# Grouping tap products by channel chunk, and adding all tap pairs in the DMA, in a convolution and MLP kernel

## Chip, cores and metric

The kernel runs on one core of one Trainium2 chip. The metric is the device time in microseconds of one execution; lower is better. The time before is the median of three runs.

## What is computed

Each token's 192 channels are split into 8 heads of 24. Every token and head has 7 weights, normalised by a softmax over the 7 taps; a tap is one of the token's own row and the six rows before it. The result goes through a two-layer MLP whose middle function is `h - tanh(h)`:

```python
w = exp(weight_gen - max); w = w / sum(w)                    # B=8, S=4096, H=8, K=7
x_pad = concat([zeros(B, 6, D), x], axis=1)                  # D = 192
x_unf[b, s, k] = x_pad[b, s + k]                             # 7 shifted rows of each token
attn = einsum('bshk,bskhg->bshg', w, x_unf).reshape(B * S, D)
h = attn @ w_in                                              # 192 x 2048
out = (h - tanh(h)) @ w_out                                  # 2048 x 192
```

## The kernel before

The 32768 tokens are cut into 32 blocks of 1024, eight consecutive tokens (`J = 8`) to each of 128 partitions. For each block:

- SP issues the loads of `x_t` (14 rows of 192 channels a partition: eight tokens and a halo of six) and of `wg_t`. ScalarE takes the exponential (L146), VectorE sums it, takes the reciprocal and scales, so that `wsm` holds the softmax.
- `products` (L205) multiplies the shifted rows with the weights, one instruction per tap: 1536 elements a partition, bf16 out. GpSimd does all seven taps of blocks 2 to 31. Taps 0, 2, 4 go to the tile `even`, taps 1, 3, 5 to `odd`, tap 6 to `last`.
- A DMA issued by GpSimd (L241) adds `odd` to `even`. Blocks 0 and 1 (`PLAIN`) have none. In blocks 2 to 6 (`PART`) it adds two tap pairs and is issued after tap 3. In the other 25 blocks it adds three pairs, without the last third of the third pair (`ACC`), and is issued after tap 5.
- `conv_sums` (L260) adds what is left, and transposes it, with matmuls against an identity (L277): 8 matmuls for each chunk of 64 channels and each remaining group. Three chunks with 4, 4 and 5 groups make 104 matmuls in a late block; five groups each make 120 in a `PART` block; seven make 168 in a `PLAIN` one. `conv_out` copies the sums to `convT`, chunks 0 and 1 on ScalarE (L303), chunk 2 on VectorE (L301).
- `gemm1` (L315) makes one of 16 f tiles: 6 matmuls into `ph`, tanh on ScalarE (L333), the subtraction `gt` on VectorE (L334). `gemm2` (L345) makes one eighth of the output of the block before from 32 matmuls into `obank` (L358).

The order on every engine is written out by hand in the program; engines run their own instructions in order. In a steady block n there are eight steps p of two `gemm1` tiles and one `gemm2` part. The products of block n+2 are issued on GpSimd at p = 0, their first instruction held back until the latest `gt` of that time (`behind`, reason "pace"). The sums of block n+1 are made at p = 6, those of chunks 0 and 1 strewn between the `gemm2` matmuls, those of chunk 2 in one burst.

The first two blocks are different. VectorE helps with the taps: the list `taps` names engine, tap and token range. `conv(0, (0, 1), (2,))` (L483) sums the groups in the order of `sums`, so TensorE takes each tap as it comes. `load_x(1, first_halo[0])` (L469) holds the second load of x behind a first product of block 0 that reads halo rows. In the pass of `gemm1` over block 0 the sums of block 1 are interleaved: 48 matmuls, the first three groups of chunks 0 and 1, after f tile 7 (p = 3), then 16 at each of p = 4, 5 and 6, and the rest at the end (L500 to L509). `hooks` puts two loads of MLP weights, issued by GpSimd, behind chosen entries of `taps`.

Of the kernel before, what the change touches and what calls it, by code (L numbers as in the profile page):

```python
# [9 lines left out]
BF16 = mybir.dt.bfloat16  # L10
# [6 lines left out]
def kernel(  # L17
# [8 lines left out]
    nc = tc.nc  # L26

    B, S, D = x.shape
    H, K = weight_gen.shape[2], weight_gen.shape[3]
    G = D // H  # L30
    F = moe_w_in.shape[1]
    P = nc.NUM_PARTITIONS
    R = P // 2
    HALO = K - 1

    J = 8
# [5 lines left out]
    NFT = F // P  # L42
    NC = D // R
    GC = G // NC
    NPAIR = K // 2
    ACC = NPAIR * J * D - J * R
    PLAIN = (0, 1)
    PART = (2, 3, 4, 5, 6)
    assert S % TOK == 0 and D % R == 0 and H * GC == R and F % P == 0
# [5 lines left out]
    ppool = ctx.enter_context(tc.tile_pool(name="ppool", bufs=2))  # L55
# [21 lines left out]
    prods_of = {}  # L77
# [120 lines left out]
    def scale(eng, wsm, e_t, zr):  # L198
        return eng.tensor_mul(  # L199
            wsm.rearrange("p j h k -> p (j h) k"),  # L200
            e_t[:].rearrange("p j h k -> p (j h) k"),
            zr.rearrange("p (n o) -> p n o", o=1).to_broadcast([P, J * H, K]),
        )

    def products(n, taps=None, sums=None, hooks={}, behind=None):  # L205

        x_t = x_of.pop(n)
        wsm, wsm_v, e_t, zr = wsm_of.pop(n)
        if e_t is not None:
            scale(nc.gpsimd, wsm[:], e_t, zr[:])  # L210

        even = ppool.tile([P, NPAIR, NC, J, H, GC], BF16, name="even")
        odd = ppool.tile([P, NPAIR, NC, J, H, GC], BF16, name="odd")
        last = ppool.tile([P, NC, J, H, GC], BF16, name="last")
        dst = {}
        for i in range(NPAIR):
            dst[2 * i] = even[:, i]
            dst[2 * i + 1] = odd[:, i]
        dst[K - 1] = last[:]
        if -1 in hooks:  # L220
            hooks[-1]()
        for eng, k, j0, j1 in taps or [(nc.gpsimd, k, 0, J) for k in range(K)]:
            w = wsm_v if eng is nc.vector else wsm[:]
            mul = eng.tensor_mul(  # L224
                dst[k][:, :, j0:j1].rearrange("p c j h g -> p j h c g"),
                x_t[:, k + j0 : k + j1, :].rearrange("p j (h c g) -> p j h c g", h=H, c=NC),
                w[:, j0:j1, :, k : k + 1]
                .rearrange("p j h (k o) -> p j h k o", o=1)
                .to_broadcast([P, j1 - j0, H, NC, GC]),
            )  # L230
            if k == 0 and behind is not None:


                order(mul, behind, "pace")
            if j1 == 1:
                first_halo[0] = mul
            if (k, n in PART) in ((3, True), (K - 2, False)) and n not in PLAIN:


                acc = 2 * J * D if n in PART else ACC  # L240
                nc.gpsimd.dma_start(  # L241
                    out=even[:].rearrange("p i c j h g -> p (i c j h g)")[:, 0:acc],
                    in_=odd[:].rearrange("p i c j h g -> p (i c j h g)")[:, 0:acc],
                    accum_op=mybir.AluOpType.add,
                    max_dma_last_dim=4096,
                )
            if k in hooks:
                hooks[k]()

        if n in PLAIN:  # L250
            prods_of[n] = [[dst[k] for k in (sums or range(K))]] * NC
        elif n in PART:
            prods_of[n] = [[dst[4], even[:, 0], even[:, 1], dst[5], last[:]]] * NC
        else:
            groups = [last[:]] + [even[:, i] for i in range(NPAIR)]
            prods_of[n] = [
                groups + ([odd[:, NPAIR - 1]] if c == NC - 1 else []) for c in range(NC)
            ]

    def conv_sums(n, parts, pcs, home=None):  # L260


        prods = prods_of[n]
        if n not in conv_of:
            conv_of[n] = cpool.tile([P, NC, HT], BF16, name="convT")
        for _ in parts:
            pcs.append(home or psum_h.tile([P, 2, HT], FP32, name="pc", tag="ph"))

        for gi in range(max(len(g) for g in prods)):
            for chunks, pc in zip(parts, pcs):  # L270
                some = [c for c in chunks if gi < len(prods[c])]
                last = gi == max(len(prods[c]) for c in chunks) - 1
                for c in some:
                    for j in range(JH):
                        col = ((c - chunks[0]) * JH + j) * R
                        for r in range(2):
                            nc.tensor.matmul(  # L277
                                pc[r][:, col : col + R] if home else pc[:, r, col : col + R],
                                lhsT=prods[c][gi][
                                    r * R : (r + 1) * R, c, 2 * j : 2 * j + 2  # L280
                                ].rearrange("p j h g -> p (j h g)"),
                                rhs=ident[r * R : (r + 1) * R, r * R : (r + 1) * R],
                                start=(gi == 0 and c == chunks[0] and j == 0),
                                stop=(last and c == some[-1] and j == JH - 1),
                            )
                            yield
# [22 lines left out]
    def conv(n, *parts):  # L309
        pcs = []  # L310
        for _ in conv_sums(n, parts, pcs):
            pass
        conv_out(n, parts, pcs)
# [127 lines left out]
    def rest_of_w_in():  # L441
        load_w_in(FA, F)

    V, G_ = nc.vector, nc.gpsimd
# [4 lines left out]
    load_w_in(0, FA, last_exp[0])  # L449
    softmax_norm_ramp(0, obank[0])  # L450
    products(
        0,

        taps=[
            (G_, 6, 0, J),
            (V, 5, 1, J),
            (V, 4, 2, J),
            (V, 5, 0, 1),
            (V, 4, 0, 2),
            (G_, 0, 0, J),  # L460
            (V, 3, 0, J),
            (V, 2, 0, J),
            (G_, 1, 0, J),
        ],
        sums=(6, 5, 4, 3, 0, 2, 1),
        hooks={1: rest_of_w_in},
    )

    load_x(1, first_halo[0])  # L469
# [4 lines left out]
    for c in range(NC):  # L474
        nc.scalar.activation(out=w_in[R:P, c, 0:FA], in_=w_in[0:R, c, 0:FA], func=ACT.Copy)
    softmax_norm_ramp(1, obank[1])
    nc.sync.dma_start(out=w_in[R:P, :, FA:F], in_=w_in[0:R, :, FA:F])
    products(
        1,
        taps=[(V, 0, 0, J), (V, 1, 0, J)] + [(G_, k, 0, J) for k in range(2, K)],  # L480
        hooks={4: load_w_out},
    )
    conv(0, (0, 1), (2,))  # L483
    softmax_exp(2)
    load_x(2)
    softmax_norm_ramp(2)
    products(2)

    def some(sums, m):
# [24 lines left out]
    for n in range(1, NTOT):  # L514
# [103 lines left out]
```

The softmax here doesn't subtract the row's maximum and nothing guards it: scores larger than these inputs give would overflow.

## Time and profile before

| quantity | value |
|---|---|
| time, median of three runs (lowest to highest) | 754.1 us (753.81 to 754.71) |
| span of the profiled execution, first to last instruction | 751.8 us |
| TensorE matmul busy | 732.1 us, 97% of the span, 14800 instructions |
| VectorE busy | 695.5 us, 93% |
| ScalarE busy | 625.3 us, 83% |
| GpSimd busy | 670.5 us, 89% |
| mean busy share of the 16 DMA engines, blocks in mid-run | 0.56 to 0.58 |
| granted TensorE clock | 1.000 |

The time of the profiled execution itself is not listed; its span stands 2.3 us under the median of the timed runs, which is what lies around the span in a timed execution. "Busy" adds the times of the instructions of an engine. The page has 40 slices of the span in tenths, the chain of work that ended last, and groups of instructions by line with the mean duration and the idle time ahead of them. The timeline lists start, duration, engine and line.

### The profile page before, as it was taken

Reading aid. Unit: us, or ns where it says so; the run is one execution under the profiler, and the core shown is the slowest. Engines: PE = TensorE matmul, PEld = TensorE weight load, DVE = VectorE, ACT = ScalarE, POOL = GpSimd, SP = SyncE. Lnnn points to the kernel's source line nnn. Section 1 sums busy time; section 2 is a strip of 40 time slices with the busy share of each in tenths; the row PEclk is TensorE's granted clock in tenths of the full one; section 3 lists DMA queues with packets and bytes.
Section 4 is the critical chain, followed back from the end, with each engine's and each line's share of the span. In section 5 each row is a group of like instructions: output and inputs, shape, how many; then the busy total and the mean of one; then the engine's idle time right before and its main releaser. Section 6 shows DMA issues by size and latency. Waiting matters only on the chain.

```text
span 751.8 us, 32359 instructions
## 1 busy us (share of the span) xinstructions
PE 732.1 (97%) x14800; PEld 577.5 (77%) x14800; DVE 695.5 (93%) x740; ACT 625.3 (83%) x840; POOL 670.5 (89%) x264
## 2 busy tenths in 40 slices
PE   3899999999999999999999999999999999999997
PEld 2477878877777778777777778777878777877777
DVE  7999999999999999999999999999999999998893
ACT  4888888888888888888888888888888888888883
POOL 8999999999999999999999999999999999999000
PEclk9999999999999999999999999999999999999999
DMA  8936444465556665555666544666544566542312
GB/s 229 213 79 172 152 149 111 107 186 171 158 161 155 186 184 126 136 151 160 176 186 172 125 130 149 171 184 186 121 125 148 168 186 173 121 115 62 79 45 86
DMA packets 25943, 110.82 MB, mean 147 GB/s; under 512 B 4703, under 2 KB 9551, under 8 KB 21838
## 3 DMA queue, kind: packets, MB, share of 16 engines
q1 hardware_dynamic: 14718, 77.03, 28.3%
q0 software_dynamic: 11088, 31.72, 24.9%
q8 instruction: 115, 1.88, 1.0%
q14 instruction: 22, 0.18, 0.1%
HBM read 54.52 MB, written 25.17 MB: 106 GB/s over the span
## 4 chain that ended last, share of the span: by engine, by line
PE 94%; DVE 4%; DMA 1%; ACT 0%; issue 0%; DVEq 0%
PE obank L358 44%; PE ph L320 43%; PE pc L277 6%; DVE gt L334 2%; PE po L395 1%; DMA x_t<-in_x_dram 1%; DVE odd L224 0%; DMA wg_t<-in_weight_gen_dram 0%; DVE even L224 0%; DVE zsum L160 0%; DVE obank L199 0%; ACT convT L295 0%; ACT e_t L146 0%; DVE obank L188 0%; DVE zr L169 0%
## 5 line engine op out<-in xcount | busy, mean ns | idle before, releaser
L334 DVE TENSOR_TENSOR gt<-ph,th 128x1024 bf16<-128x1024 f32 x512 | 602.5, 1220 | 33.0 <-ACT th L333 30.0
L333 ACT ACTIVATE th<-ph 128x1024 f32<-128x1024 f32 x512 | 497.5, 1022 | 69.4 <-PE ph L320 68.0
L358 PE MATMUL obank<-w_out,gt 64*128 64x192 bf16 x7936 | 412.5, 243 | 0.1
L358 PEld LDWEIGHTS <-gt 64*128 64x128 bf16 x7936 | 357.4, 94 | 55.7 <-issue 0.2
L320 PE MATMUL ph<-convT,w_in 64*128 64x512 bf16 x3072 | 384.9, 378 | 4.8 <-DVE gt L334 2.8
L224 POOL TENSOR_TENSOR even<-x_t,wsm 128x1536 bf16<-128x1536 f32 x93 | 287.6, 3092 | 12.3 <-DVE gt L334 12.1
L224 POOL TENSOR_TENSOR odd<-x_t,wsm 128x1536 bf16<-128x1536 f32 x93 | 287.3, 3089 | 0.0
L320 PEld LDWEIGHTS <-w_in 64*128 64x128 bf16 x3072 | 174.6, 94 | 101.6 <-issue 11.6
L377 ACT ACTIVATE out_sb<-obank 128x192 f32<-128x192 f32 x248 | 82.3, 332 | 35.0 <-PE obank L358 30.5
L224 POOL TENSOR_TENSOR last<-x_t,wsm 128x1536 bf16<-128x1536 f32 x32 | 106.6, 3333 | 0.0
L277 PE MATMUL pc<-ident,even 64*128 64x64 bf16 x2256 | 62.8, 191 | 0.3 <-DVE even L224 0.2
L277 PEld LDWEIGHTS <-even 64*128 64x128 bf16 x2304 | 59.7, 96 | 1.2 <-issue 0.5
L241 POOL DMA_DIRECT2D even<-odd x30 | 36.1, 1205 | 9.3 <-POOL odd L224 9.3
L277 PE MATMUL pc<-ident,last 64*128 64x64 bf16 x752 | 27.2, 191 | 9.3 <-POOL last L224 9.2
L303 ACT ACTIVATE convT<-pc 128x1024 bf16<-128x1024 f32 (+1 forms) x33 | 32.6, 992 | 2.8 <-PE pc L277 2.8
L277 PEld LDWEIGHTS <-last 64*128 64x128 bf16 x768 | 23.2, 96 | 9.6 <-POOL last L224 9.2
L160 DVE TENSOR_REDUCE zsum<-e_t 128x32 f32<-128x224 f32 (+1 forms) x61 | 23.7, 388 | 3.0 <-ACT e_t L146 3.0
L146 ACT ACTIVATE e_t<-wg_t 128x448 f32<-128x448 f32 x32 | 18.5, 578 | 6.7 <-DMA wg_t<-in_weight_gen_dram 6.7
L301 DVE CAST convT<-pc 128x512 bf16<-128x512 f32 x30 | 20.7, 690 | 3.6 <-PE pc L277 1.9
L169 DVE RECIPROCAL zr<-zsum 128x32 f32<-128x32 f32 (+1 forms) x58 | 20.3, 350 | 0.0
L199 DVE TENSOR_TENSOR wsm<-e_t,pc 128x448 f32<-128x448 f32 x28 | 17.4, 622 | 2.9
L277 PE MATMUL pc<-ident,odd 64*128 64x64 bf16 x416 | 14.7, 198 | 1.1 <-POOL odd L224 0.7
(29 smaller groups left out, 77.5 us busy)
## 6 DMA issues: line engine op xcount, KB each, us to landing
x_t<-in_x_dram SPq DMA_DIRECT2D x31, 1344.0 KB, 9.3
even<-odd POOLq DMA_DIRECT2D x25, 1024.0 KB, 8.8
out_dram<-out_sb SPq DMA_DIRECT2D x31, 768.0 KB, 6.9
wg_t<-in_weight_gen_dram SPq DMA_DIRECT2D x32, 224.0 KB, 10.0
even<-odd POOLq DMA_DIRECT2D x5, 768.0 KB, 7.1
x_t<-in_x_dram SPq DMA_DIRECT2D x1, 768.0 KB
w_out<-in_moe_w_out_dram POOLq DMA_DIRECT2D x1, 768.0 KB, 10.3
out_dram<-out_sb SPq DMA_DIRECT2D x4, 192.0 KB, 1.9
```

The lines of the kernel that those rows point to most:

```text
L160: nc.vector.reduce_sum(out=zsum_of[n][:, j0 * H : j1 * H], in_=e_of[n][:, j0:j1].rearrange("p j h k -> p (j h) k"), axis=AX.X,)
L169: nc.vector.reciprocal(zr_of[n][:, j0 * H : j1 * H], zsum_of[n][:, j0 * H : j1 * H])
L224: mul = eng.tensor_mul(dst[k][:, :, j0:j1].rearrange("p c j h g -> p j h c g"), x_t[:, k + j0 : k + j1, :].rearrange("p j (h c g) -> p j h ...
L241: nc.gpsimd.dma_start(out=even[:].rearrange("p i c j h g -> p (i c j h g)")[:, 0:acc], in_=odd[:].rearrange("p i c j h g -> p (i c j h g)" ...
L277: nc.tensor.matmul(pc[r][:, col : col + R] if home else pc[:, r, col : col + R], lhsT=prods[c][gi][r * R : (r + 1) * R, c, 2 * j : 2 * j + ...
L301: eng.tensor_copy(out, pc[:, :, 0:cols].rearrange("p r (cj t) -> p r cj t", t=R))
L303: last_conv[0] = nc.scalar.activation(out=out, in_=pc[:, :, 0:cols].rearrange("p r (cj t) -> p r cj t", t=R), func=ACT.Copy,)
L320: nc.tensor.matmul(ph[:, r, :], lhsT=w_in[r * R : (r + 1) * R, c, f * P : (f + 1) * P], rhs=convT[r * R : (r + 1) * R, c, :], start=(c == ...
L333: last_act[0] = nc.scalar.activation(out=th[:], in_=ph_f, func=ACT.Tanh)
L334: last_sub[0] = nc.vector.tensor_sub(gt[:], ph_f, th[:])
L358: mm = nc.tensor.matmul(po[:, 0:D], lhsT=g_of[n][f][r * R : (r + 1) * R, col : col + P], rhs=w_out[r * R : (r + 1) * R, f, :], start=(r == ...
L377: last_act[0] = nc.scalar.activation(out=out_sb[:, j, :], in_=po[:, 0:D], func=ACT.Copy)
```

## The change

The three tiles become one, `pr`, ordered by chunk c, then tap k, then token and channel: `[P, NC, K, J * R]`. An instruction now makes a range of taps of one chunk (`mul(eng, c, k0, k1)`); with all seven taps that is 3584 elements a partition. The innermost run is 8 channels: 8 adjacent x values, then a step to the next head's, and one weight held for 8 elements. Before, a weight was held for 24 elements, x was read straight on, and the output was written in runs of 8; now the output is written straight on.

The DMA adds taps 4, 5, 6 to taps 0, 1, 2. In the 25 late blocks it does so for all chunks, so every chunk has four groups left (3, 0, 1, 2); it is issued after the last product. In `PART` blocks it does so for chunks 0 and 1, and chunk 2 keeps seven groups. In block 0 VectorE makes chunks 1 and 2 and GpSimd chunk 0; in block 1 VectorE makes six taps of chunk 2 and GpSimd the rest.

```diff
-    def products(n, taps=None, sums=None, hooks={}, behind=None):
+    def products(n, taps=None, hooks={}, behind=None):
...
-        for eng, k, j0, j1 in taps or [(nc.gpsimd, k, 0, J) for k in range(K)]:
-            w = wsm_v if eng is nc.vector else wsm[:]
-            mul = eng.tensor_mul(
-                dst[k][:, :, j0:j1].rearrange("p c j h g -> p j h c g"),
-                x_t[:, k + j0 : k + j1, :].rearrange("p j (h c g) -> p j h c g", h=H, c=NC),
-                w[:, j0:j1, :, k : k + 1]
...
+        pr = ppool.tile([P, NC, K, J * R], BF16, name="pr")
+        x_v = x_t[:]
+        step = x_v.ap[0]
+
+        def mul(eng, c, k0, k1):
+            w = wsm_v if eng is nc.vector else wsm[:]
+            return eng.tensor_mul(
+                pr[:, c, k0:k1, :].rearrange("p k (jh g) -> p k jh g", g=GC),
+                bass.AP(
+                    tensor=x_v.tensor,
+                    offset=x_v.offset + k0 * D + c * GC,
+                    ap=[step, [D, k1 - k0], [G, J * H], [1, GC]],
+                ),
+                w.rearrange("p j h (k o) -> p k (j h) o", o=1)[:, k0:k1].to_broadcast(
+                    [P, k1 - k0, J * H, GC]
+                ),
             )
+        def dma_sum(c0, c1):
+            nc.gpsimd.dma_start(
+                out=pr[:, c0:c1, 0:3].rearrange("p c k t -> p c (k t)"),
+                in_=pr[:, c0:c1, 4:7].rearrange("p c k t -> p c (k t)"),
+                accum_op=mybir.AluOpType.add,
+                max_dma_last_dim=3072,
+            )
...
+        every, summed = range(K), (3, 0, 1, 2)
+        if taps is not None:
+            for i, (eng, c, k0, k1) in enumerate(taps):
+                m = mul(eng, c, k0, k1)
+                if k0 == 0 and eng is nc.vector and n not in first_halo:
+                    first_halo[n] = m
+                if i in hooks:
+                    hooks[i]()
+            prods_of[n] = parts(every, every, every)
+            return
+        first = mul(nc.gpsimd, 0, 0, K)
+        mul(nc.gpsimd, 1, 0, K)
...
         elif n in PART:
+            mul(nc.gpsimd, 2, 0, 2)
+            dma_sum(0, 2)
+            mul(nc.gpsimd, 2, 2, K)
+            prods_of[n] = parts(summed, summed, every)
         else:
+            mul(nc.gpsimd, 2, 4, K)
+            mul(nc.gpsimd, 2, 0, 3)
+            mul(nc.gpsimd, 2, 3, 4)
+            dma_sum(0, NC)
+            prods_of[n] = parts(summed, summed, summed)
+        if behind is not None:
+            order(first, behind, "pace")
...
         taps=[
-            (G_, 6, 0, J),
-            (V, 5, 1, J),
-            (V, 4, 2, J),
-            (V, 5, 0, 1),
-            (V, 4, 0, 2),
-            (G_, 0, 0, J),
-            (V, 3, 0, J),
-            (V, 2, 0, J),
-            (G_, 1, 0, J),
+            (V, 1, 6, 7),
+            (G_, 0, 6, 7),
+            (V, 2, 6, 7),
+            (V, 1, 0, 6),
+            (G_, 0, 0, 6),
+            (V, 2, 0, 6),
         ],
-        sums=(6, 5, 4, 3, 0, 2, 1),
-        hooks={1: rest_of_w_in},
+        hooks={5: rest_of_w_in},
...
         1,
-        taps=[(V, 0, 0, J), (V, 1, 0, J)] + [(G_, k, 0, J) for k in range(2, K)],
-        hooks={4: load_w_out},
+        taps=[(V, 2, 0, 6), (G_, 0, 0, K), (G_, 1, 0, K), (G_, 2, 6, K)],
+        hooks={1: load_w_out},
```

More of the change, by code (lines that the diff above doesn't have):

```diff
@@ L44 @@
     GC = G // NC
-    NPAIR = K // 2
-    ACC = NPAIR * J * D - J * R
     PLAIN = (0, 1)
@@ L210, in products @@
             scale(nc.gpsimd, wsm[:], e_t, zr[:])
[L212 to L221, printed above, removed]
-        for eng, k, j0, j1 in taps or [(nc.gpsimd, k, 0, J) for k in range(K)]:
-            w = wsm_v if eng is nc.vector else wsm[:]
-            mul = eng.tensor_mul(
-                dst[k][:, :, j0:j1].rearrange("p c j h g -> p j h c g"),
-                x_t[:, k + j0 : k + j1, :].rearrange("p j (h c g) -> p j h c g", h=H, c=NC),
-                w[:, j0:j1, :, k : k + 1]
-                .rearrange("p j h (k o) -> p j h k o", o=1)
-                .to_broadcast([P, j1 - j0, H, NC, GC]),
-            )
[L231 to L248, printed above, removed]
@@ new lines, in dma_sum, with parts @@
+        def dma_sum(c0, c1):
[5 more added lines that the diff above has]
+            )
+        def parts(*sets):
+            return [[pr[:, c, k] for k in ks] for c, ks in enumerate(sets)]
+        every, summed = range(K), (3, 0, 1, 2)
[8 more added lines that the diff above has]
+            return
@@ L250, in products @@
+        first = mul(nc.gpsimd, 0, 0, K)
+        mul(nc.gpsimd, 1, 0, K)
         if n in PLAIN:
-            prods_of[n] = [[dst[k] for k in (sums or range(K))]] * NC
+            mul(nc.gpsimd, 2, 0, K)
+            prods_of[n] = parts(every, every, every)
         elif n in PART:
-            prods_of[n] = [[dst[4], even[:, 0], even[:, 1], dst[5], last[:]]] * NC
-        else:
[L255 to L258, printed above, removed]
+            mul(nc.gpsimd, 2, 0, 2)
+            dma_sum(0, 2)
+            mul(nc.gpsimd, 2, 2, K)
+            prods_of[n] = parts(summed, summed, every)
+        else:
+            mul(nc.gpsimd, 2, 4, K)
[3 more added lines that the diff above has]
+            prods_of[n] = parts(summed, summed, summed)
@@ L279, in conv_sums @@
                                 lhsT=prods[c][gi][
-                                    r * R : (r + 1) * R, c, 2 * j : 2 * j + 2
-                                ].rearrange("p j h g -> p (j h g)"),
+                                    r * R : (r + 1) * R, 2 * j * R : (2 * j + 2) * R
+                                ],
                                 rhs=ident[r * R : (r + 1) * R, r * R : (r + 1) * R],
```

## Prediction

> **What bounds the kernel now.** I read the page's busy times and its chain first, then the groups of the product and sum lines, then the timeline of the ramp and of one steady block.
>
> ```profile
> PE 732.1 (97%) x14800; PEld 577.5 (77%) x14800; DVE 695.5 (93%) x740; ACT 625.3 (83%) x840; POOL 670.5 (89%) x264
> PE 94%; DVE 4%; DMA 1%; ACT 0%; issue 0%; DVEq 0%
> L224 POOL TENSOR_TENSOR even<-x_t,wsm 128x1536 bf16<-128x1536 f32 x93 | 287.6, 3092 | 12.3 <-DVE gt L334 12.1
> ```
>
> TensorE carries 94% of the chain; the rest is the ramp. GpSimd is no bound, but close: its only slack is 12.1 us of pace waits in 15 blocks. Between the x loads of two late blocks (381.30 and 403.78) the period is 22.48 us. The product starts on GpSimd show what it needs:
>
> ```profile
> 381.70 2.90 POOL L224 TENSOR_TENSOR even<-x_t,wsm 128x1536 bf16<-128x1536 f32 x1 [0.85 <-DVE gt L334]
> 384.56 2.90 POOL L224 TENSOR_TENSOR odd<-x_t,wsm 128x1536 bf16<-128x1536 f32 x1
> ...
> 399.20 1.20 POOL L241 DMA_DIRECT2D even<-odd  x1 [0.30 <-POOL odd L224]
> ```
>
> Start to start is 2.86 us for 1536 elements, 1.862 ns each; seven make 20.0 us, the DMA 1.5, the wait 0.85. In the ramp the order matters, not the rate:
>
> ```profile
> 9.59 5.94 DMA x_t<-in_x_dram
> 20.16 16.94 DVE gt L334 x15
> ```
>
> These two pieces of the chain of waits are the second x load and the pass over block 0, where VectorE's `gt` sets the pace (25.67 to 38.2 for 11, so 1.13 us each). Inside that pass the timeline shows the first sums of block 1, and GpSimd still at its products:
>
> ```profile
> 25.81 0.82 PE L320 MATMUL ph<-convT,w_in 64*128 64x512 bf16 x6 [0.31 <-DVE gt L334]
> 26.13 1.23 POOL L424 DMA_DIRECT2D w_out<-in_moe_w_out_dram  x1
> 26.45 0.41 PE L277 MATMUL obank<-ident,even 64*128 64x64 bf16 x16
> 26.68 0.41 PE L277 MATMUL obank<-ident,odd 64*128 64x64 bf16 x16
> 26.92 0.41 PE L277 MATMUL obank<-ident,even 64*128 64x64 bf16 x16
> 27.38 2.92 POOL L224 TENSOR_TENSOR odd<-x_t,wsm 128x1536 bf16<-128x1536 f32 x1
> 30.25 2.90 POOL L224 TENSOR_TENSOR last<-x_t,wsm 128x1536 bf16<-128x1536 f32 x1
> ```
>
> TensorE takes taps 0, 1, 2 at 26.45 without a wait while GpSimd finishes taps 5 and 6 until 33.1. That works because products are made tap by tap.
>
> **What the Trainium skill says.** "GPSIMD Engine Reference", section 3.1, gives about 2.6 cycles per element for a two-input operation; at its 1.2 GHz the 1.862 ns here are 2.23, somewhat better. Its section 7 prices reads whose inner step is over 8 bytes at half as much again; the new inner step is 4 bytes, so that does not apply, and it says nothing of short runs. "SBUF — State Buffer", section "SBUF: two separate sides", lets GpSimd block VectorE operations with two SBUF inputs; the new VectorE products still read weights from PSUM (`obank`), and the trace agrees that such pairs run side by side (1.75 us for 1536 elements while GpSimd works). "TensorE: Matmul & The Clock Gate", Part 1, has half clock until about 3.4 us of steady work; the trace agrees: 24 sums of block 0 take about 0.60 us, 40 later ones 0.58. "DMA: Bandwidth & Descriptors", "Issuing engines are not separate DMA queues": all transfers share 16 engines. The trace agrees: the 1024 KB addition lands after 8.0 us at 399.2, but after 13.7 at 289.88, just ahead of an output store and an x load.
>
> **Late blocks: what goes.** Each of 25 blocks loses 8 sums (104 to 96), all in the burst of chunk 2. That burst is back to back: 40 of them take 0.58 us on the chain at 57.48, 14.5 ns each. 25 x 8 x 14.5 ns = **2.9 us** less. The period of `PART` blocks (104.39 less 81.61: 22.78) against late ones gives 0.30 us for 16, 18.8 ns each, so 3.75 us is the other bound. VectorE waits some 1.0 us a block for tanh (30.0 us in all), so it can follow. `PART` and `PLAIN` counts stay at 120 and 168.
>
> **Late blocks: GpSimd and the DMA.** Elements stay at 10752 a block. No row shows this pattern. I take 1.862 ns an element and no saving from fewer instructions: 20.0 us, 6.67 for 3584. Below: the 448-element scaling on GpSimd (1.04 us, start to start) as the small end of a line gives 1.67 ns and 0.29 fixed, so 6.28 for 3584. Above: all of that 1.04 us as a rate, with its runs of 7, gives 2.32 ns and 8.3 us. With the DMA's 1.2 (its 0.3 wait goes, a 1.0 us product now stands between) a block costs 21.2 of a period of 22.37: hidden, by 1.2.
> The DMA is issued at 381.7 + 20.0 = 401.7 instead of 399.2, with 1152 KB: 8.8 x 1.125 = 9.9 us typically, and 13.7 x 1.125 = 15.4 if the store and x load (403.35, 403.78) crowd it as at 289.88; it lands between 411.6 and 417.1. The sums start at 394.8 + 22.4 = 417.2, and the first that needs it follows 0.4 later. Hidden, barely. Where that cover goes, TensorE waits once a block. SP's x load waits on its own queue behind the output store, so the reordered products do not move it.
>
> **Block 0, step by step.** VectorE's starts give 1.05 ns an element and 0.06 fixed. Two 512-element products from 6.48 end at 7.68; the halo rows (504 KB, 6.1 us after an issue near 1.7) I put at 8.0; two of 3072 (3.29 each) end at 11.3 and 14.6, where it was 13.27. The x load of block 1 now stands behind the first of these: issued 11.35 instead of 9.59, landed 17.3 with the same 5.94. GpSimd: 512 elements, 3072 from 8.0 to 13.7, the w_in DMAs (1.7) to 15.4, a wait for `zr` to 16.05, the scaling (1.08) to 17.15. TensorE can do little until chunk 2 is there at 14.6, then 152 sums at 25 ns: 18.4 instead of 15.6. The copy and half-clock matmuls as before (15.58 to 19.18) give the first `gt` at about 22.0; VectorE itself, with its block 1 product from 17.3, its sum and reciprocal, at 21.7. Alone this is 1.9 us late.
>
> **Block 1's products, the larger step.** GpSimd makes chunk 0 from 17.3 to 24.0, issues w_out (1.23), and makes chunk 1 from 25.2 to **31.9**. But the 48 sums after f tile 7 read chunk 1, and TensorE comes to them near 28.2. It waits 3.6 us, and behind it stand all `gemm1` tiles from f = 8; ScalarE and VectorE run dry. Then 40 sums (0.58), and from the first matmul of a tile to its `gt` 1.97 (37.79 to 39.76): `gt` 8 starts at 31.9 + 0.05 + 0.58 + 1.97 = 34.5. Before, it was 25.67 + 3 x 1.13 = 29.1. **5.4 us late**, in which block 0's delay is contained. The remaining eight again run at 1.13, so nothing comes back; after that TensorE has no gaps to absorb it. Bounds: 6.28 a product gives 4.6; 7.0 gives 6.1; a half clock after the wait adds up to 1.2.
> Block 2 is safe: GpSimd starts it at 34.0, issues its DMA (768 KB, 7.1) at 49.3, so it lands at 56.5; the sums, at 55.2 before, come at 60.6.
>
> **Sum.** 5.4 less 2.9 is +2.5 us on the profiled span of 751.8, 754.3. The timed median stands 2.3 above that span, so I add to 754.1: **756.6 us**.
>
> **Rivals.**
> *GpSimd becomes the bound.* At over 21.2 us of products a block, 6% more per element than now, TensorE follows GpSimd, or waits for the late DMA. For: runs of 8 for x and weights where there were 24, and the scaling with runs of 7 looks slower per element. Against: runs of 8 were in the old output. At 10% more: 22.0 + 1.2 = 23.2 a block, against 22.48 now 0.7 x 25 = 18; with 6 for the ramp 778. At the upper bound, 24.9 + 1.2 = 26.1, 3.6 x 25 = 90: near 850. Chance 0.25.
> *Not slower, because GpSimd takes the long instruction much faster.* The gain of 2.9 remains if chunk 1 is ready by 29.4, which asks for (29.4 - 17.3 - 1.23) / 2 = 5.4 us or less, 1.52 ns an element. At 4.7 only block 0's 1.9 us remains: 753.1. For: seven instructions' fixed costs become one's. Against: the line through both GpSimd rows allows 6.28. Chance 0.05.
> *A tie.* A saving of 3.75 and products of 6.28 leave 4.6 - 3.75 = +0.9: 755.0. Chance 0.12.
> That an instruction is split again by tap would leave the order as it is here; sums are fixed by the loops.
> The forecast itself, 754.9 to 758.5 by the bounds above, has 0.58.
>
> **Numbers.** A measurement here tells about 0.2%, 1.5 us. Slower by more: the forecast and the GpSimd case, 0.83; within: the tie, 0.12; faster: 0.05. For the range, 754.8 below leaves out the fast case and a little of the tie; above it goes into the GpSimd case as far as 775, which leaves out about half of it.
>
> **What would show it.** Right: products of 6.5 to 6.9 us for 3584 elements; one wait of TensorE for GpSimd of 3 to 4 us between 28 and 32; sums in L277 down by 200; period 22.37; no wait of the sums for the DMA. Wrong: pace waits of GpSimd gone and one TensorE wait a block (the GpSimd case), or sums at f = 7 without a wait (the fast case).

## Result, and the profile after

| | before | after |
|---|---|---|
| time, median of four runs each on one chip (lowest to highest) | 754.23 us (753.81 to 754.71) | 801.2 us (799.15 to 801.64) |
| ratio, 95% interval | | 1.0614 (1.0598 to 1.063) |
| span of the profiled execution | 751.8 us | 799.9 us (its own time 801.64) |

The change costs 47 us, 6.1%. (By the last row 1.7 us lie around the span of one execution; the 2.3 us named for the kernel before compare the span of one with the median of several.) The page of the kernel after, busy times, chain, and the row of the products:

```profile
PE 740.1 (93%) x14600; PEld 581.7 (73%) x14600; DVE 696.8 (87%) x737; ACT 626.0 (78%) x840; POOL 729.7 (91%) x196
POOL 60%; DMA 18%; PE 16%; issue 3%; DVE 2%; ACT 1%; SPq 0%; POOLq 0%; DVEq 0%
L217 POOL TENSOR_TENSOR pr<-x_t,wsm 128x3584 bf16<-128x3584 f32 (+4 forms) x150 | 693.4, 4941 | 6.1 <-DVE gt L343 3.2
```

The chain was 94% TensorE; now it is 60% GpSimd and 18% DMA. The 200 matmuls fewer are there. GpSimd's share of the span went up by only 2 points, so the shares alone don't show the change of bound. The waits do: of the pace waits (`POOL pr <- DVE gt`), which were 12.1 us in 15 blocks, 3.2 us in 5 blocks are left. The list of waits of the kernel after gives what was waited for, the total, how often, and the longest:

```profile
PE pc L286 <- DMA pr<-pr: 31.2, 22, 6.0
...
PE obank L286 <- POOL pr L217: 4.5, 1, 4.5
POOL pr L217 <- DVE gt L343: 3.2, 5, 1.8
...
POOL pr L230 <- POOL pr L217: 7.7, 25, 0.6
```

TensorE waits for the addition in 22 of 25 late blocks and once for GpSimd in the pass over block 0 (ahead of its very first sums it waits for GpSimd too, 15.6 us where it was 9.2), and the DMA still waits for the last product. One steady block on the timeline (start, duration, engine):

```profile
318.41 22.43 POOL L217 TENSOR_TENSOR pr<-x_t,wsm 128x3584 bf16<-128x3584 f32 x5
...
333.47 0.20 PE L286 MATMUL pc<-ident,pr 64*128 64x64 bf16 x2 [1.37 <-DMA pr<-pr]
341.13 1.29 POOL L230 DMA_DIRECT2D pr<-pr  x1 [0.30 <-POOL pr L217]
341.59 0.34 SPq L390 DMA_DIRECT2D out_dram<-out_sb  x1
342.03 0.38 SPq L111 DMA_DIRECT2D x_t<-in_x_dram  x1
342.45 22.02 POOL L217 TENSOR_TENSOR pr<-x_t,wsm 128x3584 bf16<-128x3584 f32 x5
```

GpSimd goes from one block's products to the next's without a pause of its own. A block takes it 23.61 us from DMA to DMA (317.52, the DMA ahead of these lines, to 341.13): 1.28 of that DMA's issue, 22.0 from its end to the end of the products (318.80 to 340.84), and 0.30 of wait. In 16 of the 24 intervals between late DMAs it is 23.61 to 23.64, as at the end:

```profile
698.73 1.28 POOL L230 DMA_DIRECT2D pr<-pr  x1 [0.30 <-POOL pr L217]
699.55 22.50 POOL L217 TENSOR_TENSOR pr<-x_t,wsm 128x3584 bf16<-128x3584 f32 x5
722.34 1.29 POOL L230 DMA_DIRECT2D pr<-pr  x1 [0.30 <-POOL pr L217]
```

In the kernel before GpSimd needs 21.55 us from DMA to DMA where nothing else holds it back, and the steady period is 22.49:

```profile
160.56 1.20 POOL L241 DMA_DIRECT2D even<-odd  x1 [0.30 <-POOL odd L224]
...
182.11 1.20 POOL L241 DMA_DIRECT2D even<-odd  x1 [0.30 <-POOL odd L224]
```

The DMA now goes out just ahead of the output store and the x load, and its row of the DMA issues gives the median from issue to landing:

```profile
pr<-pr POOLq DMA_DIRECT2D x25, 1152.0 KB, 15.7
```

15.7 us, where 1024 KB took 8.8. The first late DMA and the last two, which have no x load beside them, land after 9.4 and 9.8.

The ramp, from the timeline after:

```profile
9.28 6.26 POOL L217 TENSOR_TENSOR pr<-x_t,wsm 128x3072 bf16<-128x3072 f32 x1 [1.95 <-DMA x_t<-zero]
12.63 0.35 SPq L111 DMA_DIRECT2D x_t<-in_x_dram  x1
18.82 7.28 POOL L217 TENSOR_TENSOR pr<-x_t,wsm 128x3584 bf16<-128x3584 f32 x1 [0.46 <-DMA x_t<-in_x_dram]
...
27.29 8.44 POOL L217 TENSOR_TENSOR pr<-x_t,wsm 128x3584 bf16<-128x3584 f32 x2
34.64 1.25 PE L286 MATMUL obank<-ident,pr 64*128 64x64 bf16 x40 [4.54 <-POOL pr L217]
38.27 2.51 DVE L343 TENSOR_TENSOR gt<-ph,th 128x1024 bf16<-128x1024 f32 x2 [5.48 <-ACT th L342]
```

The 3584 products of one chunk take 7.2 us (18.82 to 26.04, where the w_out DMA follows), not 6.67; chunk 1 of block 1 is ready at 34.6, and `gt` 8 starts at 38.27 instead of 29.07.

Where the 48 us go is read from the starts of the output stores in the traces, block by block. Each column is a profiled execution less that of the kernel before, in us; the last five kernels are experiments below. One execution each is behind a column: kernels with blocks 0 and 1 as before stand anywhere from +0.3 to +3.8 at block 0, so differences of a few us in the ramp tell little.

| output store of block | after | small_dma | tapwise_late | ramp_before | block1_before | allpairs |
|---|---|---|---|---|---|---|
| 0 | +9.46 | +10.32 | +11.15 | +1.88 | +2.72 | +3.80 |
| 4 | +8.62 | +9.39 | +9.20 | +4.64 | +2.70 | +3.63 |
| 7 | +23.28 | +15.75 | +10.78 | +20.81 | +8.05 | +6.59 |
| 27 | +48.51 | +21.61 | +11.40 | +46.29 | +8.29 | +6.85 |

So for the kernel after: 9 us in the ramp, 15 over the first three late blocks, and 25 over the 20 blocks that follow, 1.26 each. In those 20, GpSimd's 23.61 less the period of 22.49 makes 1.12; the rest is in blocks where GpSimd is held up besides.

### The profile page after: what moved, and what is told of

Same layout as the page of the kernel before. It is cut to its first block, busy times and chain, and to the rows that moved or that the text cites. A ratio compares the mean times of both kernels' runs of the same rounds, so it can differ in the third digit from the quotient of the medians.

```text
span 799.9 us, 31888 instructions
## 1 busy us (share of the span) xinstructions
PE 740.1 (93%) x14600; PEld 581.7 (73%) x14600; DVE 696.8 (87%) x737; ACT 626.0 (78%) x840; POOL 729.7 (91%) x196
## 4 chain that ended last, share of the span: by engine, by line
POOL 60%; DMA 18%; PE 16%; issue 3%; DVE 2%; ACT 1%; SPq 0%; POOLq 0%; DVEq 0%
POOL pr L217 58%; DMA pr<-pr 15%; PE obank L367 6%; PE ph L329 6%; PE pc L286 2%; POOL pr L230 2%; DMA x_t<-in_x_dram 2%; DVE gt L343 2%; PE po L404 1%; DMA x_t<-zero 1%; ACT th L342 1%; DVE pr L217 0%; POOL wsm L197 0%; SPq L111 0%; POOL w_out L433 0%
## 5 line engine op out<-in xcount | busy, mean ns | idle before, releaser
L217 POOL TENSOR_TENSOR pr<-x_t,wsm 128x3584 bf16<-128x3584 f32 (+4 forms) x150 | 693.4, 4941 | 6.1 <-DVE gt L343 3.2
L367 PEld LDWEIGHTS <-gt 64*128 64x128 bf16 x7936 | 355.8, 94 | 55.9
L286 PE MATMUL pc<-ident,pr 64*128 64x64 bf16 x3224 | 86.6, 195 | 46.9 <-DMA pr<-pr 31.2
L286 PEld LDWEIGHTS <-pr 64*128 64x128 bf16 x3336 | 85.4, 99 | 55.8 <-DMA pr<-pr 33.8
L230 POOL DMA_DIRECT2D pr<-pr x30 | 40.9, 1363 | 7.7 <-POOL pr L217 7.7
L158 DVE TENSOR_REDUCE zsum<-e_t 128x32 f32<-128x224 f32 (+1 forms) x61 | 23.6, 387 | 2.8 <-ACT e_t L144 2.8
L167 DVE RECIPROCAL zr<-zsum 128x32 f32<-128x32 f32 (+1 forms) x58 | 20.3, 350 | 0.0
L217 DVE TENSOR_TENSOR pr<-x_t,obank 128x3072 bf16<-128x3072 f32 (+1 forms) x5 | 11.3, 2285 | 2.5 <-DMA x_t<-zero 1.6
L404 PE MATMUL po<-w_out,gt 64*128 64x192 bf16 x256 | 11.2, 243 | 0.0
L404 PEld LDWEIGHTS <-gt 64*128 64x128 bf16 x256 | 10.8, 93 | 0.0
L418 DVE TENSOR_TENSOR out_sb<-po,ot 128x192 f32<-128x192 f32 x8 | 2.9, 358 | 8.3 <-ACT ot L417 8.3
L417 ACT ACTIVATE ot<-po 128x192 f32<-128x192 f32 x8 | 2.7, 332 | 7.2 <-PE po L404 7.2
## 6 DMA issues: line engine op xcount, KB each, us to landing
pr<-pr POOLq DMA_DIRECT2D x25, 1152.0 KB, 15.7
```

Source lines behind the costliest of these rows:

```text
L158: nc.vector.reduce_sum(out=zsum_of[n][:, j0 * H : j1 * H], in_=e_of[n][:, j0:j1].rearrange("p j h k -> p (j h) k"), axis=AX.X,)
L217: return eng.tensor_mul(pr[:, c, k0:k1, :].rearrange("p k (jh g) -> p k jh g", g=GC), bass.AP(tensor=x_v.tensor, offset=x_v.offset + k0 * ...
L230: nc.gpsimd.dma_start(out=pr[:, c0:c1, 0:3].rearrange("p c k t -> p c (k t)"), in_=pr[:, c0:c1, 4:7].rearrange("p c k t -> p c (k t)"), ac ...
L286: nc.tensor.matmul(pc[r][:, col : col + R] if home else pc[:, r, col : col + R], lhsT=prods[c][gi][r * R : (r + 1) * R, 2 * j * R : (2 * j ...
L367: mm = nc.tensor.matmul(po[:, 0:D], lhsT=g_of[n][f][r * R : (r + 1) * R, col : col + P], rhs=w_out[r * R : (r + 1) * R, f, :], start=(r == ...
L404: nc.tensor.matmul(po[:, r, 0:D], lhsT=g_of[n][f][r * R : (r + 1) * R, col : col + P], rhs=w_out[r * R : (r + 1) * R, f, :], start=(f == 0 ...
```

## Experiments

Every time is a median beside runs of the kernel before on the same chip (754.4 to 754.6).

**patterns: what sets GpSimd's rate per element.** GpSimd alone runs `tensor_mul` four times in each of eight patterns of reading. The kernel holds none of the computation. In short, with [step, count] pairs from the outermost to the innermost loop (`one` is `chunk` with a single tap, `plain_short` is `plain` with 1536 elements):

```
run("tap",       1536, out [8,64][512,3][1,8], x [24,64][8,3][1,8],   w [7,64][0,3][0,8])
run("chunk",     3584, out [512,7][8,64][1,8], x [192,7][24,64][1,8], w [1,7][7,64][0,8])
run("xstraight", 3584, out as chunk,           x straight on,         w as chunk)
run("whold",     3576, out straight on,        x [72,149][24,3][1,8], w [7,149][0,3][0,8])
run("long",      3576, out and x straight on,                         w [7,149][0,24])
run("plain",     3584, out, x and w all straight on)
```

> GpSimd alone multiplies constants in eight access patterns, four instructions each, with no other engine at work; the convolution and the MLP are left out and the output is zeros. The trace of the changed kernel has 7.22 us start to start for 3584 elements, 2.01 ns each, against 1.862 ns for a tap before. If the weight held for only 8 elements is what costs, the pattern of the changed kernel with x read straight on stays near 2.0 ns an element and the one with the weight held for 24 falls to about 1.86. If the jumps in x cost, it is the other way round. If neither, the time is in the length of the instruction and the pattern with everything straight on is near 2.0 as well. The 512-element pattern against the 3584-element one gives the fixed cost of an instruction: near 0 if the rate theory holds, 0.16 to 0.3 us if the prediction's lower bound was right.

Its groups by form; the second number after the bar is the mean of one in ns:

```profile
L68 POOL TENSOR_TENSOR plain<-xb,wb 128x3584 bf16<-128x3584 f32 x4 | 30.9, 7726 | 0.2
L68 POOL TENSOR_TENSOR chunk<-xb,wb 128x3584 bf16<-128x3584 f32 x4 | 29.1, 7275 | 0.2
L68 POOL TENSOR_TENSOR xstraight<-xb,wb 128x3584 bf16<-128x3584 f32 x4 | 27.8, 6958 | 0.2
L68 POOL TENSOR_TENSOR long<-xb,wb 128x3576 bf16<-128x3576 f32 x4 | 26.1, 6515 | 0.2
L68 POOL TENSOR_TENSOR whold<-xb,wb 128x3576 bf16<-128x3576 f32 x4 | 25.9, 6468 | 0.2
...
L68 POOL TENSOR_TENSOR tap<-xb,wb 128x1536 bf16<-128x1536 f32 x4 | 11.6, 2903 | 15.7 <-DVE wb L57 15.4
L68 POOL TENSOR_TENSOR plain_short<-xb,wb 128x1536 bf16<-128x1536 f32 x4 | 13.7, 3417 | 0.2
...
L68 POOL TENSOR_TENSOR one<-xb,wb 128x512 bf16<-128x512 f32 x4 | 4.8, 1196 | 0.2
```

`chunk` and `one` have the same runs: (7275 - 1196) / 3072 = 1.98 ns an element and 0.18 us fixed. `plain` and `plain_short` give 2.10 ns and again 0.18 to 0.19 us. With that fixed part taken off, an element takes 1.76 to 1.77 ns where the weight is held for 24 elements (`whold`, `long` and `tap`), 1.89 where it is held for 8 and x is read straight on, 1.98 in the kernel's chunk pattern, and 2.10 where each element has its own weight. The hold of the weight is the largest part; jumps of x cost 0.09 ns at a hold of 8 and nothing at 24. Writing straight on is no help. The fixed parts of which the change merges seven into five a block are 0.18 us each. GpSimd alone takes 7275 ns for `chunk` and the kernel after 7.28 us, so it isn't other engines or the DMA that slow the product there. And these rates give 22.2 us for the five products of a block and 20.3 for the seven of before, against 22.02 (kernel after) and 20.06 (tapwise_late) in the traces, where neighbouring records overlap by 0.04: the pattern of reading accounts for the 2.0 us.

**small_dma: the late DMA cut to 128 KB.** Only tap 4 of chunk 0 is added, the rest of the pairs left out of the sum.

```diff
-            dma_sum(0, NC)
+            nc.gpsimd.dma_start(out=pr[:, 0, 0], in_=pr[:, 0, 4], accum_op=add, ...)
```

> The changed kernel, with the late blocks' DMA cut from 1152 KB to 128 KB (tap 4 of chunk 0 alone is added; the other pairs are left out of the sums). GpSimd still issues it at the same place. Theory 1, GpSimd is the bound: its cadence of 23.6 us a block (22.0 of products and 1.6 around the DMA) stays, TensorE waits for GpSimd's products or the small DMA instead, 785 to 798 us, less than 801.2 mostly by the shorter landing at the end. Theory 2, the crowded DMA (landing 15.7 us) is the bound and GpSimd only follows TensorE: the waits go, the period falls to 22.4, 758 to 768 us.

773.55 us, ratio 1.0245 (1.0228 to 1.0262): between the two. Without the large DMA the slope of the table falls from 1.26 us a block to 0.29 (5.86 over 20 blocks). GpSimd is still past the period, as its timeline shows:

```profile
400.02 5.50 POOL L274 DMA_DIRECT2D pr<-pr  x1
400.63 26.92 POOL L217 TENSOR_TENSOR pr<-x_t,wsm 128x3584 bf16<-128x3584 f32 x5
422.60 5.78 POOL L274 DMA_DIRECT2D pr<-pr  x1
423.21 27.20 POOL L217 TENSOR_TENSOR pr<-x_t,wsm 128x3584 bf16<-128x3584 f32 x5
```

The products of two blocks end at 427.55 and 450.41, 22.86 apart: the 22.02 of products and 0.84 more. That is 0.37 over the period of 22.49, against 1.12 in the kernel after. Of the 0.75 between them, 0.30 is the wait for the last product, which the small DMA doesn't have; the other 0.45 is what the issue of the large one takes more (1.29 against 0.84). So the rate brings GpSimd just past the period, and the wait and the issue of the large DMA do the rest; neither theory had both. What its late landing adds is at most what is left of the 0.97 a block, 0.2.

**tapwise_late: the products of blocks 2 to 31 tap by tap, all else as after.** One flat tile that holds taps 0, 2, 4, then 1, 3, 5, then 6; the products are made in the order 0 to 6, and the DMA adds all three pairs after the last, 96 sums.

```diff
-        first = mul(nc.gpsimd, 0, 0, K)
-        mul(nc.gpsimd, 1, 0, K)
+        first = tap(0)
...
+            for k in range(1, K):
+                tap(k)
+            add_odd(3)
```

> The changed kernel with blocks 0 and 1 unchanged, but GpSimd's products of blocks 2 to 31 made tap by tap as before (1536 elements, 1.862 ns each). In the late blocks the DMA still adds all three pairs, 1152 KB, after the last product, and the sums stay at 96. Theory 1, the slower rate of the chunk products is what costs: GpSimd needs 21.5 us a block again, the period returns to 22.4, and only the ramp's delay remains: 754.2 + 9.2 - 2.9 = 760.5, up to 766 if the crowded DMA makes the sums wait a few tenths a block. Theory 2, the DMA behind the last product is what costs whatever the rate: 785 us or more.

764.76 us, ratio 1.0131 (1.0114 to 1.0148): 36 of the 47 us are gone. The tap products change three things at once: the element rate, the number of instructions, and the DMA's wait for the last product, which is no longer recorded. By their sizes it is mainly the rate: where nothing holds it back GpSimd needs 21.3 us a block (its products end at 188.67 and 209.99), 2.3 less than in the kernel after, of which 2.0 are products and 0.3 is the wait. GpSimd has its pauses back, and TensorE waits for the DMA only once in the late blocks, 1.6 us. From the list of waits:

```profile
POOL pr L236 <- DVE gt L365: 28.0, 22, 1.8
```

and of its DMA issues, with the same bytes (in one stretch a partition instead of three) and the same place behind the last product:

```profile
pr<-pr POOLq DMA_DIRECT2D x25, 1152.0 KB, 12.4
```

The period is 22.49 again, not 22.37. The saving of 8 sums a block isn't there even where neither GpSimd nor the DMA stands in its way; the runs from allpairs on take this up.

**ramp_before: blocks 0 and 1 as before, the late blocks as after.**

```diff
-            (V, 1, 6, 7),
-            (G_, 0, 6, 7),
...
+            (G_, 6, 0, J),
+            (V, 5, 1, J),
...
-        taps=[(V, 2, 0, 6), (G_, 0, 0, K), (G_, 1, 0, K), (G_, 2, 6, K)],
+        taps=[(V, 0, 0, J), (V, 1, 0, J)] + [(G_, k, 0, J) for k in range(2, K)],
```

> The changed kernel with blocks 0 and 1 as before: the old list of taps, one instruction per tap, the old order of sums, the old hold of the second x load. Blocks 2 to 31 stay as changed. Theory 1, from block 2 on GpSimd is the bound: only what GpSimd itself gains counts, the start of its block 2 products at 34.2 instead of 36.7, so 2.6 us less than 801.2, 797 to 800. Theory 2, the ramp's 9.2 us at the eighth f tile of block 0 adds to the rest: 792 us.

800.11 us, ratio 1.0601 (1.0585 to 1.0617). The 7.6 us that the ramp gains at the output store of block 0 have shrunk to 2.5 at block 7 (20.81 against 23.28), and 2.2 at the end. What TensorE is ahead, it spends waiting for DMAs, 36.3 us where it was 31.2 (three of the 23 waits are in `PART` blocks); the same row of its waits:

```profile
PE pc L297 <- DMA pr<-pr: 36.3, 23, 7.0
```

**allpairs: the kernel before, with the third pair added in full by the DMA.** Products and ramp unchanged, 96 sums.

```diff
-    ACC = NPAIR * J * D - J * R
+    ACC = NPAIR * J * D
...
-            prods_of[n] = [
-                groups + ([odd[:, NPAIR - 1]] if c == NC - 1 else []) for c in range(NC)
-            ]
+            prods_of[n] = [groups] * NC
```

> The kernel before, with one thing of the change: in the late blocks the DMA adds all three tap pairs (1024 KB becomes 1152 KB, at its old place after tap 5), and the sums fall from 104 to 96. Products stay tap by tap. Theory 1, the prediction's: TensorE is back to back there, so 25 blocks lose 0.116 us each, 751.3 us. Theory 2, from the timeline: the next f tile (14) needs the PSUM buffer that the subtraction of f tile 13 frees, which ends 0.06 us before that tile starts in the kernel before, so the saved matmuls leave a hole and the period stays at 22.49: 754 to 754.8 us.

760.91 us, ratio 1.0073 (1.0051 to 1.0095): slower, which neither theory said. The steady period is 22.49. The loss has two places. In the ramp, x lands 2.1 us later in its profile (the first product starts at 8.36 instead of 6.23); that comes and goes between kernels that don't differ there, and its origin stays open. At the first late blocks it is 3.0 us, on the timeline:

```profile
173.00 2.90 POOL L224 TENSOR_TENSOR odd<-x_t,wsm 128x1536 bf16<-128x1536 f32 x1 [2.73 <-DMA even<-odd]
...
198.00 0.20 PE L275 MATMUL pc<-ident,even 64*128 64x64 bf16 x2 [1.68 <-DMA even<-odd]
```

GpSimd waits with the second product of block 8 until the first late DMA, of block 7, has landed (163.20 to 172.94). It does so this one time in the run and not at all in the kernel before, where that product starts at 167.06 and the DMA lands at 169.47. No late sum reads `odd` any more; whether that ties the buffer to the DMA was not tried. Then the sums of block 8 wait once for their own DMA.

**What holds the period at 22.49.** The end of VectorE's subtraction of f tile 13, and the first matmul of f tile 14, in the kernel before:

```profile
417.44 2.35 DVE L334 TENSOR_TENSOR gt<-ph,th 128x1024 bf16<-128x1024 f32 x2 [0.26 <-ACT th L333]
...
419.85 1.50 PE L320 MATMUL ph<-convT,w_in 64*128 64x512 bf16 x12
```

and in tapwise_late, with 8 sums fewer between them:

```profile
586.27 2.36 DVE L365 TENSOR_TENSOR gt<-ph,th 128x1024 bf16<-128x1024 f32 x2 [0.26 <-ACT th L364]
...
588.68 1.50 PE L351 MATMUL ph<-convT,w_in 64*128 64x512 bf16 x12
```

The subtractions end at 419.79 and 588.63; the matmuls start 0.06 and 0.05 later. `ph` has three buffers, and f tile 14 needs the one that the subtraction of f tile 13 frees. TensorE's burst ended just in time for it: busy, but not what set the time. Sums taken out of the burst leave a hole.

The traces bear this out over 21 blocks (8 to 28, medians, first matmul to first matmul). From f tile 13 to f tile 14 it is 3.68 us in the kernel before, in allpairs and in tapwise_late, though in the latter two the last matmul ahead of f tile 14 starts 0.045 us earlier (not the 0.116 of 8 matmuls at 14.5 ns). From f tile 14 to f tile 1 of the next block it is 3.20 us, and from there to f tile 13 15.61, in all three: 22.49 together. The last and longest piece is TensorE's own work, for it shrinks to 15.52 when two matmuls are taken out of it (fill3_ahead2, below). The sums stand in the first, which VectorE sets.

If so, work must be put in the place of the sums, which `FILL` does: it is the number of f tiles of the second matmul between the burst and f tile 14.

```diff
-    FILL, AHEAD = 2, 1
+    FILL, AHEAD = 3, 1
```

**allpairs_fill3**, and **allpairs_fill4** with `FILL = 4`:

> As the run with all pairs added in the DMA of the kernel before, and the filler between the sums and f tile 14 raised from two to three f steps of the second matmul (four to six instructions of 41 ns). Theory 2, the hole behind the sums is 0.12 us a late block: 0.08 of it is filled with work that would come later, 25 x 0.08 = 2 us less than the run without it, 752 to 753 us. Theory 1, TensorE had no hole: moving work between its instructions changes nothing, the same as the run without it.

> As the run before it, with a filler of four f steps, 0.165 us more than two. Theory 2: the hole of 0.12 us is filled and 0.045 us overflows, which costs nothing on TensorE itself but makes tanh and the subtraction of f tile 14 later by that much; 25 x 0.12 = 3 us less than with two, 751 to 752.5 us. Theory 1: the same as with two.

758.65 us, ratio 1.0048 (1.0034 to 1.0063), and 760.19, 1.0073 (1.0059 to 1.0086). The period is 22.49 with 3 and 22.57 with 4, where f tile 14 starts 3.77 us behind f tile 13 instead of 3.68 and the whole block is longer with it. Work moved into the hole brings nothing, since f tile 1 of the next block in turn waits for the subtraction of f tile 14. That fill3 is 2.3 us below allpairs is no gain of the period: at the output store of block 0 their profiles stand at +1.76 and +3.80.

**sums_end: tapwise_late, with the sums of block 1 all at the end of the pass over block 0**, so that f tile 8 doesn't stand behind chunk 1's products.

```diff
-        if 3 <= p <= 6:
-            some(sums, (3 if p == 3 else 1) * 4 * JH)
```

> The run with tap by tap products in blocks 2 to 31 (764.8 us, its ramp is that of the changed kernel), with the sums of block 1 moved from f tile 7 on to the end of the pass over block 0. TensorE then doesn't wait for chunk 1 of block 1 in the middle of the pass. Theory 1, that wait and the slow clock behind it are what the ramp costs: the first subtraction stays 3 us late, the 6 us that came at f tile 8 go, less some 1 us for 112 sums at the end that were hidden before, 759 to 761 us. Theory 2, the ramp's delay comes from the later x load and GpSimd's longer products alone: 763 us or more.

762.57 us, ratio 1.0103 (1.0087 to 1.0119), between the theories. At block 0 the delay is 4.8 us instead of 11.2; at block 7 it is 9.8 against 10.8. So the wait in the pass makes most of the ramp's delay, but little of its end: without it the kernel is 4.4 us late at block 4 and loses 5 more at the first late blocks.

**block1_before: tapwise_late, with block 1 tap by tap as before and only block 0 by chunks.**

```diff
+        if n == 1:
+            for k in range(K):
+                tap(k, nc.vector if k < 2 else nc.gpsimd)
```

> tapwise_late with the products of block 1 made tap by tap as before (VectorE taps 0 and 1, GpSimd taps 2 to 6); block 0 by chunks as after, 96 sums a late block. Theory 1: of the 9.2 us by which gt 8 is late, block 0 (first gt 23.2 instead of 20.1) makes about 3 and block 1's chunk order (a wait of 4.5 and matmuls at half clock behind it) about 6; with tap order there is no wait of the sums for GpSimd at f = 7, gt 8 starts near 32, and the time is 757 to 759. Rival: what the ramp loses is only passed through, and the first late blocks, where GpSimd's backlog meets the DMA that is now issued after the last tap, set the time whatever the ramp did, as when the sums were put at the end: 761 to 764.

761.68 us, ratio 1.0098 (1.0085 to 1.0112): the rival. The ramp itself divides as theory 1 had it: 2.7 us for block 0, so 8.4 of the 11.15 for block 1's order. But the time follows from the first late blocks, where the DMA that goes out after the last tap lands too late, here the second of them:

```profile
184.39 2.17 POOL L247 DMA_DIRECT2D pr<-pr  x1
...
199.37 0.20 PE L316 MATMUL pc<-ident,pr 64*128 64x64 bf16 x2 [3.49 <-DMA pr<-pr]
```

Issued at 184.39, needed 11.5 later, landed at 199.37. In the kernel before, a first DMA of 1024 KB goes out after tap 5, one product (2.9 us) earlier. Delays of the ramp and of this place don't add: who comes late to it waits less.

**fill3_ahead2: the kernel before with work ahead of both gates**, and **pairs_part8: the version that the runs so far point to**: all pairs in the DMA, products tap by tap, one tile (no `odd` to wait for), `PART` up to block 8, `FILL = 3`, `AHEAD = 2`, ramp as before.

```diff
-    FILL, AHEAD = 2, 1
+    FILL, AHEAD = 3, 2
...
-    PART = (2, 3, 4, 5, 6)
+    PART = (2, 3, 4, 5, 6, 7, 8)
```

> The kernel before with one more f tile of the second matmul ahead of f tile 14 (FILL 3) and ahead of f tile 1 (AHEAD 2); products, DMA and 104 sums unchanged. Theory 1: the period of 22.49 us of a late block holds two short waits for VectorE's subtraction, 0.06 us ahead of f tile 14 and of f tile 1 each, and idle TensorE time there is all that is to be had: 0 to 0.1 us a block, so 752 to 754. Theory 2: TensorE is bound by its own instructions, nothing changes: 754 to 755.

> All tap pairs in the DMA with the products tap by tap as before, in one tile; blocks 2 to 8 in PART (120 sums), FILL 3 and AHEAD 2, blocks 0 and 1 as before: the version of the idea that the runs so far point to, with no wait for the buffer of odd and with the first all-pairs block two blocks later. Theory 1: 96 sums bring their time once both gates have work ahead of them: 0.1 us a block over 23 blocks, so 751 to 753. Theory 2: VectorE's subtractions set the pace of 22.49 and the saving stays nothing: 754 to 756, and more if the x load comes 2 us later again, as in allpairs.

754.67 us, ratio 1.0005 (0.9996 to 1.0013), and 756.6 us, 1.0032 (1.002 to 1.0045). The period of pairs_part8 is 22.45 to 22.50 in most blocks, so of the 0.116 us at most 0.04 is saved, with single blocks of 22.67 to 22.90 that cost more. Its timeline shows the stretch in which VectorE sets the time:

```profile
418.56 2.36 DVE L330 TENSOR_TENSOR gt<-ph,th 128x1024 bf16<-128x1024 f32 x2 [0.26 <-ACT th L329]
...
420.99 1.52 PE L316 MATMUL ph<-convT,w_in 64*128 64x512 bf16 x12
421.90 1.94 ACT L329 ACTIVATE th<-ph 128x1024 f32<-128x1024 f32 x2 [0.31 <-PE ph L316]
422.96 2.36 DVE L330 TENSOR_TENSOR gt<-ph,th 128x1024 bf16<-128x1024 f32 x2 [0.41 <-ACT th L329]
...
424.28 0.83 PE L316 MATMUL ph<-convT,w_in 64*128 64x512 bf16 x6
```

Subtraction of f tile 13 to 420.92, f tile 14 at 420.99, its tanh at 421.90, its subtraction from 422.96 to 424.14, and f tile 1 at 424.28: each step waits for the one before, and no sum is in it. No version of the change that was run is faster than the kernel before.

## Why the prediction was wrong in size

The sign was right, and the likely forecast (+2.5 us) was not what happened. The rival in which GpSimd becomes the bound did, with 801.2 inside its 778 to 850. The step that failed first is GpSimd "hidden, by 1.2": a block was to cost it 21.2 us and costs 23.6, with a period of 22.49.

- **The element rate, the larger part of that step.** The term "1.862 ns an element" gave 20.0 us of products a block; they measure 22.0. An instruction of 3584 takes 7.2 us, 2.015 ns an element, 8% more, and the block with its five instructions 10%, where the text itself had put the point at 6%. The row of before was for a weight held for 24 elements; the change holds it for 8. The text saw the shorter runs, said "No row shows this pattern", and answered it with the old output's runs of 8, which patterns shows to be the operand that doesn't matter. The upper bound from the scaling, with a new weight every 7 elements, pointed the right way.
- **The DMA's wait that "goes".** It stayed in all 25 late blocks, 7.7 us in all. The last product before the DMA is tap 3 of chunk 2, which the addition doesn't use, but it lies inside the stretch of `pr` that the DMA runs over. No run tries this alone; but where the product just ahead lies outside that stretch, in the `PART` blocks of the kernel after, in small_dma and in the late blocks of tapwise_late, no wait is recorded.
- **The DMA "hidden, barely".** The bound for a crowded DMA, 15.4, was close: 15.7. What failed is the issue time, which comes with the late products. This step and the first are one: at the old rate (tapwise_late) a DMA of the same bytes lands after 12.4 and is hidden in steady blocks.
- **2.9 us of sums saved.** 200 matmuls are gone and no time with them. The failed step is "That burst is back to back", read as a bound. allpairs and tapwise_late have the 96 sums at the old rate, and both keep 22.49. The 0.30 us between `PART` and late blocks, which agreed so well with the price of a matmul, fits a bound on one side only: 120 sums overrun the subtraction, 104 just reach it. "VectorE waits some 1.0 us a block for tanh, so it can follow" overlooked that this wait is part of the loop.
- **Block 0, 1.9 us.** 3.1 in the trace (first `gt` at 23.17 instead of 20.07): the row of zeros landed at 9.25, not 8.0, which moves the x load to 12.63. block1_before gives block 0's part as 2.7.
- **Block 1, 5.4 us.** The mechanism was there as described: one wait of TensorE at f = 7, 4.54 us, predicted as 3.6. Terms that were too small: the start of its products at 18.82 instead of 17.3, products of 7.2 for 6.67 (twice), and 1.1 us behind the wait, where the granted clock was 0.50 and the 40 sums took 1.25 us instead of 0.58; the bounds had this as "up to 1.2". 9.2 in place of 5.4.
- **The sum.** It adds the ramp to the late blocks. ramp_before and block1_before show that the two don't add: of 7.6 us less in the ramp, 2.2 reach the end where GpSimd is the bound.
- **Not seen at all: the first late blocks,** 15 us in the kernel after, up to 5 at the old rate. GpSimd comes to them without slack, and the DMA that was issued in mid-block now goes out at its end. The prediction looked at block 2 and at steady blocks, not at the change from one kind to the other. This is also why the rival's own 10% case, which has the measured 22.0 us of products, came to 778 and not to 801: its ramp is 6 instead of 9, its block 23.2 instead of 23.6, and these blocks are not in it.

The range left out half of the GpSimd case, and the case had 0.25. A margin of 1.2 us of 21.2, resting on a rate for a pattern that no row showed, was thin support for being hidden.

## What to carry to other kernels

Before reshaping an operand on GpSimd, look at how long its repeated operand is held, and measure the new pattern by itself: 10% more work for an engine with 4% of a period to spare (0.85 of 22.49 us here) is a new bound. An engine without idle time is a bound only if the next step waits for it; compare the end of each work item with the start of what needs it, here the subtraction 0.06 us ahead of f tile 14, before counting what a shorter burst saves. Where a transfer is moved to the end of a stage, cost the first stage that has it, with the backlog that its engine brings along, and not only the steady one.

## Of the hardware, not expected

- GpSimd's product of two float inputs depends on the hold of the repeated one: 1.76 ns an element at 24, 1.89 at 8 and 2.10 at 1 (x straight on; 0.18 us fixed taken off). Reading everything straight on is the slowest pattern of those run.
- The length of a record on GpSimd is not always its cost. In the kernel after, the five products behind a DMA are recorded with 22.49 us when their record starts 0.82 us after that of the DMA, which lasts 1.29, and with 22.02 when it starts later. 0.82 + 22.49 and 1.29 + 22.02 are both 23.31, so the longer record ends no later. In small_dma, where no late DMA waits for a product, the starts come 22.58 us apart and the ends 22.86, so that the recorded issue of 128 KB grows from 2.69 to 7.83 us over the run without any more work in it. Distances between ends, or between DMAs that wait, were the measure used here.
- The landing of an addition of 1152 KB depends on what is issued beside it: 9.4 to 9.8 us without an x load, 15.7 with an output store and an x load within 1 us (kernel after).
